# Attention and two MLP layers on one core: one column of the MLP moved out of the attention phase for the first two blocks, and another order of the loads

## The chip, the core and the metric

The kernel runs on one core of one Trainium2 chip. The metric is the time of one execution in microseconds (us) on the device, as the median of several runs. One further execution is taken with the hardware profiler; all durations below come from it.

The engines are TensorE (PE: matrix products; PEld is its loading of weights), VectorE (DVE), ScalarE (ACT), GpSimd (POOL) and SyncE (SP). SP computes nothing here: it issues every transfer between HBM and the core's memory, one after another in its queue.

## What is computed

An attention over a window of 16 positions plus 24 block summaries, then two MLP layers, all in float32:

```
q, k, v: (2, 8, 768, 64)                      # sequences, heads, positions, head size
k_sum = k.reshape(B, H, 24, 32, D).max(3);  v_sum = v.reshape(B, H, 24, 32, D).mean(3)
local   = scale * q @ k.T, masked to |i - j| < 16
summary = scale * q @ k_sum.T + log(32)
a = softmax(concat(local, summary));  x = a @ concat(v, v_sum)     # -> 1536 tokens x 512
h = x @ w_in;   x = softplus(h) @ w_out           # layer 1, 512 -> 2048 -> 512
h = x @ w2_in;  out = relu(h)**2 @ w2_out         # layer 2, the same sizes
```

## The kernel before, in words

**Tiles and blocks.** The 1536 tokens are 12 tiles of 128; tiles 0 to 5 belong to the first sequence, 6 to 11 to the second. Two tiles make a block of 256 tokens. The hidden size of a layer is cut into 16 columns of 128.

**An MLP step** takes one column for one group of tokens. In `mlp_in` (line 664 is its matmul) 12 matmuls write the hidden values h; ACT and DVE apply the nonlinearity and split the result into a rounded part and a rest (g...h and g...l); in `mlp_out` (line 701) 12 matmuls add the column's share to the accumulators accp and acc. Each float32 product is made of three products of rounded numbers, hence tiles such as wih and wil, xh and xl.

**Phases.** `PH` cuts the 16 columns of a layer into three phases: columns 0 to 3, 4 to 9, 10 to 15. The first phase of layer 1, called phase A here, runs in blocks of 256 tokens while attention still runs: after each two tiles of attention the four columns of that block are queued. The text calls one column of one block an A-step. All later phases run in groups of 512 tokens (a B-step is one column of 512 tokens), and they can begin only when the whole attention is done, since their weights and accumulators lie where attention had its tiles ("late places").

**Attention of a tile t** (`tile_sc`, `tile_px`): scores on PE (line 491, into the tile sc), mask and maximum on DVE (499, 530), subtraction on POOL (532), exponential on ACT (534), sum on DVE (516 to 518), scaling on POOL (536), transposition on PE (547), product with the values in vwin on PE (561), and the splitting into xh and xl (306, 571). sc exists once, s and vwin twice (even and odd tiles).

**What attention needs per sequence.** Queries and keys are loaded in pieces of 256 KB (lines 350 and 382) and transposed on PE (361 and 397). The summaries of the keys (ks, and kaug from it) need all six pieces of the sequence's keys before the first scores of that sequence. The summaries of the values need one load of 1.5 MB into late (line 430), and 24 products on PE (line 439, `vsum_mm`). For each tile two windows of the values are loaded into vwin (line 425). In this layout a row of a query, key or window load is 256 bytes.

**Weights.** For each column two loads of 512 KB go into one of four buffers raw (lines 599 and 602). Then each is converted by four to six instructions on ACT, DVE and POOL (609, 611, 614, 306, 308, 623), which also free the buffer.

**What sets the order.** `Plan` records all operations with a due time, an estimated duration and what they need, and lays them out on the engines by a greedy list schedule before anything runs; the order on each engine is then fixed, and each engine works off its queue in order. Where the plan expects PE to be idle for long it puts matmuls without use into PE's queue (line 857); they run whether PE turns out to be idle or not. In the plan a transfer is one queue with a rate (`kb / 245.0`) and a latency.

## Time and profile before

| | us |
|---|---|
| median of 3 runs | 619.96 (619.87 to 622.35) |
| profiled execution, its own time | 620.8 |
| its span | 619.0 |
| PE busy | 602.5 (97%) |
| DVE busy | 312.1 (50%) |
| ACT busy | 288.2 (47%) |
| POOL busy | 202.0 (33%) |

The span reads in three parts. Up to about 60 us the transfers are busy all the time. From about 56 to 120 us PE and DVE are both nearly full. After that PE works without a gap to the end, apart from the last stores. Attention ends at about 132 us, phase A at about 150 us.

### The profile page before, as it was taken

Reading aid. Unit: us, or ns where it says so; the run is one execution under the profiler, and the core shown is the slowest. Engines: PE = TensorE matmul, PEld = TensorE weight load, DVE = VectorE, ACT = ScalarE, POOL = GpSimd, SP = SyncE. Lnnn points to the kernel's source line nnn. Section 1 sums busy time; section 2 is a strip of 40 time slices with the busy share of each in tenths; the row PEclk is TensorE's granted clock in tenths of the full one; section 3 lists DMA queues with packets and bytes.
Section 4 is the critical chain, followed back from the end, with each engine's and each line's share of the span. In section 5 each row is a group of like instructions: output and inputs, shape, how many; then the busy total and the mean of one; then the engine's idle time right before and its main releaser. Section 6 shows DMA issues by size and latency. Waiting matters only on the chain.

```text
span 619.0 us, 9449 instructions
## 1 busy us (share of the span) xinstructions
PE 602.5 (97%) x3809; PEld 507.5 (82%) x3809; DVE 312.1 (50%) x449; ACT 288.2 (47%) x501; POOL 202.0 (33%) x197
## 2 busy tenths in 40 slices
PE   9798999999999999999999999999999999999996
PEld 7687988999788888888888888888888888888885
DVE  5788999726664133542146652247542533232332
ACT  4686888856653124542247643346412432221220
POOL 5877696535550042331138440116000410000000
PEclk9798999999999999999999999999999999999999
DMA  9999632423541014340024330114100100010011
GB/s 283 243 281 217 162 74 55 116 69 116 166 128 35 0 35 136 103 136 1 0 64 122 120 103 0 35 61 131 47 1 0 69 0 2 0 58 11 20 50 68
DMA packets 64524, 51.34 MB, mean 83 GB/s; under 512 B 36320, under 2 KB 58848, under 8 KB 64480
## 3 DMA queue, kind: packets, MB, share of 16 engines
q1 hardware_dynamic: 64480, 50.73, 28.6%
q8 instruction: 30, 0.49, 0.3%
q14 instruction: 14, 0.11, 0.1%
HBM read 47.58 MB, written 3.15 MB: 82 GB/s over the span
## 4 chain that ended last, share of the span: by engine, by line
PE 84%; DVE 8%; DMA 4%; ACT 2%; SPq 1%; issue 1%; POOL 0%; DVEq 0%; POOLq 0%
PE h L664 40%; PE accp L701 21%; PE acc L701 18%; DMA late<-in_v_dram 2%; DMA vwin<-in_v_dram 2%; DVE raw L614 2%; DVE mx L530 1%; DVE s L499 1%; PE ab L439 1%; PE ab L561 1%; DVE sm L516 1%; SPq L382 1%; PE ab L547 1%; DVE xl L571 0%; DVE sm L517 0%
## 5 line engine op out<-in xcount | busy, mean ns | idle before, releaser
L664 PE MATMUL h<-xh,wih 128*128 128x512 f32 (+1 forms) x432 | 159.9, 370 | 0.0
L664 PE MATMUL h<-xh,wil 128*128 128x512 f32 (+1 forms) x432 | 158.7, 367 | 0.0
L664 PE MATMUL h<-xl,wih 128*128 128x512 f32 (+1 forms) x432 | 158.7, 367 | 0.0
L614 DVE SCALAR_TENSOR_TENSOR raw<-raw 128x512 uint32<-128x512 uint32 x128 | 113.3, 902 | 52.8 <-ACT raw L609 39.8
L664 PEld LDWEIGHTS h<-xh,wih 128*128 128x128 f32 x432 | 81.5, 189 | 14.6 <-issue 0.6
L664 PEld LDWEIGHTS h<-xh,wil 128*128 128x128 f32 x432 | 81.3, 188 | 13.9
L664 PEld LDWEIGHTS h<-xl,wih 128*128 128x128 f32 x432 | 81.4, 188 | 13.7
L673 ACT ACTIVATE e<-h 128x512 f32<-128x512 f32 x48 | 28.8, 599 | 125.4 <-PE h L664 125.4
L675 DVE SCALAR_TENSOR_TENSOR h<-h,e 128x512 f32<-128x512 f32 x48 | 33.5, 698 | 103.2 <-ACT e L673 103.1
L671 ACT ACTIVATE h<-h 128x512 f32<-128x512 f32 (+1 forms) x60 | 29.8, 499 | 83.2 <-PE h L664 83.1
L308 POOL TENSOR_SCALAR wih<-raw 128x512 fp32r<-128x512 f32 x18 | 12.6, 703 | 150.5 <-PE h L664 142.1
L623 POOL TENSOR_TENSOR wol<-raw,woh 128x512 fp32r<-128x512 f32 x30 | 42.6, 1421 | 48.9 <-ACT woh L306 48.3
L623 POOL TENSOR_TENSOR wil<-raw,wih 128x512 fp32r<-128x512 f32 x31 | 42.6, 1374 | 28.9 <-ACT wih L306 27.4
L609 ACT ACTIVATE raw<-raw 128x512 uint32<-128x512 uint16 x59 | 39.3, 670 | 13.2 <-DMA raw<-in_moe_w_out_dram 7.5
L680 DVE TENSOR_TENSOR g1l<-h,g1h 128x512 fp32r<-128x512 f32 (+1 forms) x40 | 24.2, 606 | 31.9 <-ACT g1h L678 31.8
L723 DVE TENSOR_TENSOR part<-accp,part 128x512 f32<-128x512 f32 x24 | 16.0, 686 | 43.5 <-PE accp L701 43.5
L680 DVE TENSOR_TENSOR g2l<-h,g2h 128x512 fp32r<-128x512 f32 x28 | 19.3, 690 | 33.7 <-ACT g2h L678 33.5
L306 ACT ACTIVATE raw<-raw 128x512 f32<-128x512 f32 x41 | 27.5, 673 | 18.7 <-DVE raw L614 18.7
L680 DVE TENSOR_TENSOR g0l<-h,g0h 128x512 fp32r<-128x512 f32 (+1 forms) x40 | 24.1, 605 | 21.1 <-ACT g0h L678 20.9
L678 ACT ACTIVATE g0h<-h 128x512 fp32r<-128x512 f32 (+1 forms) x40 | 21.2, 534 | 16.4 <-DVE h L675 16.0
L536 POOL TENSOR_TENSOR s<-s,sm 128x960 f32<-128x960 f32 (+1 forms) x14 | 22.1, 1580 | 13.9 <-DVE sm L518 13.0
L678 ACT ACTIVATE g1h<-h 128x512 fp32r<-128x512 f32 (+1 forms) x40 | 21.4, 534 | 9.2 <-DVE h L675 8.9
(172 smaller groups left out, 1175.4 us busy)
## 6 DMA issues: line engine op xcount, KB each, us to landing
raw<-in_moe_w_in_dram SPq DMA_DIRECT2D x32, 512.0 KB, 4.2
raw<-in_moe_w_out_dram SPq DMA_DIRECT2D x32, 512.0 KB, 3.4
vwin<-in_v_dram SPq DMA_DIRECT2D x20, 192.0 KB, 5.7
part<-in_k_dram SPq DMA_DIRECT2D x12, 256.0 KB, 4.9
late<-in_v_dram SPq DMA_DIRECT2D x2, 1536.0 KB, 11.3
out_dram<-part SPq DMA_DIRECT2D x12, 256.0 KB, 2.1
part<-in_q_dram SPq DMA_DIRECT2D x10, 256.0 KB, 5.1
vwin<-in_v_dram SPq DMA_DIRECT2D x4, 160.0 KB, 5.2
```

What stands on the lines that cost most here:

```text
L306: nc.scalar.activation(out=out_, in_=in_, func=AF.Copy, **({} if mul is None else {"scale": mul}))
L536: op(("POOL", "DVE"), (1.8 * n + 0.1, 1.75 * n), due, lambda e, sv=sv, rv=rv, spread=spread: tt(e).tensor_tensor(out=sv, in0=sv, in1=sprea ...
L609: nc.scalar.activation(out=lo, in_=q4[:, :, 1], func=AF.Copy, scale=2.0 ** -13, bias=-4095.5 / 8192.0)
L614: nc.vector.scalar_tensor_tensor(out=lo, in0=hi, scalar=n, in1=lo, op0=how, op1=ALU.bitwise_or)
L623: op(("POOL", "DVE"), (1.4, 1.0), dv, lambda e: tt(e).tensor_tensor(out=ws[s][kl], in0=lo.bitcast(F32), in1=ws[s][kh].bitcast(F32), op=ALU ...
L664: nc.tensor.matmul(out=hview(st), lhsT=ws[s][wn][:, w_], rhs=xx[bl][:, kk, o:o + n], start=(kk == 0 and xx is xh and wn == "ih"), stop=(kk ...
L671: op("ACT", ta, due, lambda: nc.scalar.activation(out=hview(st), in_=hview(st), func=AF.Softplus), w=[H_], tab="sp")
L673: op("ACT", ta, due, lambda: nc.scalar.activation(out=e_t[st["g"] % 2], in_=hview(st), func=AF.Relu), r=[H_], w=[("e", st["g"] % 2)])
L675: op("DVE", tv, due, lambda: nc.vector.scalar_tensor_tensor(out=hview(st), in0=hview(st), scalar=0.0, in1=e_t[st["g"] % 2], op0=ALU.max, o ...
L678: op("ACT", ta, due, lambda: nc.scalar.activation(out=gview(st)[0], in_=hview(st), func=AF.Copy), r=[H_] + need, w=gk[0])
L680: op("DVE", tv, due, lambda: nc.vector.tensor_tensor(out=gview(st)[1], in0=hview(st), in1=gview(st)[0].bitcast(F32), op=ALU.subtract), r=[ ...
L701: nc.tensor.matmul(out=o, lhsT=a[:, sl], rhs=b, start=(st["first"] and c == 0 and not (A and m % 2)), stop=(st["last"] and c == 2 and not ...
```

## The change

- `FA = (3, 3, 4, 4, 4, 4)`: in phase A blocks 0 and 1 do columns 0, 1 and 2 only. Column 3 of these 512 tokens becomes the first step of the second phase of layer 1.
- `EARLY` goes from 2 to 1: only the loads of column 0's weights get the early due time.
- `REL_K`, `REL_D`: in the plan the keys of the second sequence may not be issued before 24, 28 and 32 (the plan's own time), per pair of pieces.
- The plan's estimates of transfers change (latency, and the sizes that stand for pieces with short rows), and two copies (`vsum_put`, `mk_kaug`) go through the common helper; the copy of the value summaries may now also be put on ACT. With these the whole list schedule comes out in another order, the number of matmuls without use too.

The core of the diff (a new style "d" of the softmax in `tile_sc` and a list `KAUG_E` with POOL alone are left out: no tile uses the one, and the other is what stood there):

```diff
 PH = ((0, 4), (4, 10), (10, 16))
+FA = (3, 3, 4, 4, 4, 4)
...
-EARLY = 2
+EARLY = 1
...
+REL_K = 24.0
+REL_D = 4.0
+REL_V = 0.0
...
             if kb:
-                dma = max(dma, end + 1.6) + kb / 245.0
-                end = dma + 0.3
+                dma = max(dma, end + 1.2) + kb / 245.0
+                end = dma + 1.5
...
             for t0 in range(0, NT, n):
+
+                if L == 1 and ph < 2:
+                    f0, f1 = (0, FA[t0 // 256]) if A else (FA[t0 // 256], PH[1][1])
                 for f in range(f0, f1):
...
-        T += 24 * 0.2267 * st["n"] / 512 + (13.0 / PH[0][1] if st["A"] and st["t0"] < 1024 else 0.0)
+        T += 24 * 0.2267 * st["n"] / 512 + (13.0 / FA[st["t0"] // 256] if st["A"] and st["t0"] < 1024 else 0.0)
...
-    def ld_qk(src, u, place, due):
+    def ld_qk(src, u, place, due, rel=0.0):
...
-                w=[(place, r)], kb=285)
+                w=[(place, r)], kb=285, rel=rel)
...
-                w=[(place, z)], kb=180)
+                w=[(place, z)], kb=206)
...
-            out=PL["V"], in_=v[b].rearrange("h (p r) d -> p h r d", r=VR)), w=["V"], kb=1017)
+            out=PL["V"], in_=v[b].rearrange("h (p r) d -> p h r d", r=VR)), w=["V"], kb=1090, rel=b * REL_V)
...
-        op("POOL", 1.3, due, lambda: nc.gpsimd.tensor_scalar(
...
+        op(("POOL", "ACT"), (1.15, 1.0), due, lambda e: copy(
...
-            (ld_qk if b else ld_pair)(k, u, K_AT[u], dk - LD_K[b])
+            if b:
+                ld_qk(k, u, K_AT[u], dk - LD_K[b], REL_K + REL_D * (u - NU))
+            else:
+                ld_pair(k, u, K_AT[u], dk - LD_K[b])
...
-            run_steps(stA[nA * blocks:nA * blocks + nA], LAG_A)
+            run_steps([st for st in stA if st["t0"] == 256 * blocks], LAG_A)
```

What this does to the queues, at three places. Line numbers in rows of the changed kernel are its own: 358, 433, 438, 611 and 614 there are 350, 425, 430, 599 and 602 here on SP; 369, 447, 497 and 676 there are 361, 439, 491 and 664 here on PE. raw are weights, late is the value load for the summaries, vwin the windows of the values, part the place of queries and keys.

First, the loads of SP behind the first keys and queries. Before:

```order
L599 DMA raw_75<-in_moe_w_in_dram 128x4x256
L602 DMA raw_76<-in_moe_w_out_dram 128x1024
L599 DMA raw_77<-in_moe_w_in_dram 128x4x256
L602 DMA raw_78<-in_moe_w_out_dram 128x1024
L430 DMA late<-in_v_dram 128x8x384
```

Now:

```order
L611 DMA raw_75<-in_moe_w_in_dram 128x4x256
L614 DMA raw_76<-in_moe_w_out_dram 128x1024
L438 DMA late<-in_v_dram 128x8x384
L433 DMA vwin_130<-in_v_dram 80x8x64
L433 DMA vwin_130<-in_v_dram 96x8x64
L611 DMA raw_77<-in_moe_w_in_dram 128x4x256
```

The first value load stands behind two weight loads instead of four.

Second, further down SP's queue, up to the last key piece of the second sequence. Before (the late load here is the second sequence's):

```order
L350 DMA part_69<-in_q_dram 128x8x64 x2
L350 DMA part_70<-in_k_dram 128x8x64 x2
L350 DMA part_69<-in_q_dram 128x8x64 x2
L599 DMA raw_75<-in_moe_w_in_dram 128x4x256
L430 DMA late<-in_v_dram 128x8x384
L602 DMA raw_76<-in_moe_w_out_dram 128x1024
L599 DMA raw_77<-in_moe_w_in_dram 128x4x256
L425 DMA vwin_130<-in_v_dram 96x8x64 x2
L602 DMA raw_78<-in_moe_w_out_dram 128x1024
L350 DMA part_70<-in_k_dram 128x8x64
L425 DMA vwin_131<-in_v_dram 96x8x64 x2
L350 DMA part_70<-in_k_dram 128x8x64
```

Now:

```order
L438 DMA late<-in_v_dram 128x8x384
L358 DMA part_70<-in_k_dram 128x8x64 x2
L614 DMA raw_76<-in_moe_w_out_dram 128x1024
L433 DMA vwin_130<-in_v_dram 96x8x64 x2
L358 DMA part_70<-in_k_dram 128x8x64 x2
L611 DMA raw_77<-in_moe_w_in_dram 128x4x256
L433 DMA vwin_131<-in_v_dram 96x8x64 x2
L614 DMA raw_78<-in_moe_w_out_dram 128x1024
L358 DMA part_70<-in_k_dram 128x8x64
L611 DMA raw_75<-in_moe_w_in_dram 128x4x256
L433 DMA vwin_130<-in_v_dram 96x8x64 x2
L358 DMA part_70<-in_k_dram 128x8x64
```

All six key pieces now stand behind the value load, among the windows of tiles 2, 3 and 4, and five weight loads stand ahead of the last piece where it was four.

Third, on PE, the products for the second sequence's value summaries (ab from late and sel). Before, they stood behind the products of tile 2 with its values (ab from at and vwin):

```order
L361 MATMUL ab_141<-ident,part_69 128x128 x4
L561 MATMUL ab_142<-at_134,vwin_130 64x64 x16
L439 MATMUL ab_141<-late,sel 24x128 x24
L664 MATMUL h_108<-xh_71,wih_91 128x256
```

Now they stand before column 1 of block 0 (h_109 from wih_87), right behind column 0 and the scores of tile 4:

```order
L676 MATMUL h_108<-xh_71,wil_84 128x256
L497 MATMUL sc<-kaug_128,qT_126 64x120 x16
L369 MATMUL ab_142<-ident,part_69 128x128 x4
L447 MATMUL ab_141<-late,sel 24x128 x24
L369 MATMUL ab_142<-ident,part_70 128x128 x4
L676 MATMUL h_109<-xh_71,wih_87 128x256
```

They moved ahead of three quarters of block 0's work and of the values of tile 2.

## Rows read from the trace of the kernel before

**Rows 1.** The page's 40 slices of the span: busy tenths of the transfers.

```profile
DMA  9999632423541014340024330114100100010011
```

**Rows 2.** Stretches: length; PE, PEld, DVE, ACT, POOL busy; PE clock, DMA share, GB/s.

```profile
36.27:59.92 23.65, 20.09 (x256) 17.40 (x253) 19.27 (x30) 17.45 (x31) 17.47 (x17) 0.93 1.03 263
52.00:54.00 2.00, 2.00 (x44) 1.68 (x44) 2.00 (x2) 1.55 (x3) 1.36 (x2) 0.50 0.86 144
54.00:56.00 2.00, 2.00 (x25) 1.57 (x18) 2.00 (x4) 1.29 (x5) 1.44 (x2) 0.73 0.83 177
56.00:104.00 48.00, 45.44 (x624) 41.67 (x623) 47.30 (x66) 40.39 (x67) 38.00 (x33) 1.00 0.53 123
59.92:69.69 9.77, 9.75 (x109) 9.38 (x107) 9.70 (x15) 7.95 (x14) 6.39 (x7) 1.00 1.09 235
69.69:132.40 62.71, 59.81 (x809) 55.87 (x810) 53.25 (x78) 51.53 (x84) 42.16 (x33) 1.00 0.29 71
149.70:613.00 463.30, 462.73 (x2048) 380.79 (x2047) 194.31 (x271) 179.92 (x307) 105.57 (x90) 1.00 0.17 56
```

**Rows 3.** The chain that ended last: start us, us, what.

```profile
28.65 0.44 PE ab L361 x4
...
31.20 0.44 PE h L547 x4
...
36.51 1.44 PE h L664 x12
...
38.31 12.58 DMA vwin<-in_v_dram
...
107.54 0.98 PE sc L491 x32
...
111.59 1.44 PE accp L701 x12
...
191.68 2.72 PE h L664 x12
194.40 1.36 PE accp L701 x6
```

**Rows 4.** Timeline of PE: start us, us, operation [idle before <-releaser].

```profile
22.00 2.78 PE L439 MATMUL ab<-late,sel 128*24 128x128 f32 x48 [3.33 <-DMA late<-in_v_dram]
...
36.27 0.36 PE L664 MATMUL h<-xh,wih 128*128 128x256 f32 x1
...
57.30 0.93 PE L857 MATMUL h<-ident 128*128 128x256 bf16 x7
...
58.83 1.15 PE L561 MATMUL ab<-at,vwin 120*64 120x64 f32 x32
```

**Rows 5.** Timeline of SP's queue: start us, us, line and load issued.

```profile
35.24 0.46 SPq L430 DMA_DIRECT2D late<-in_v_dram  x1
```

**Rows 6.** Transfers from 20 to 60: GB/s in 40 slices; issues, KB, landing us.

```profile
GB/s 179 167 200 109 228 197 209 242 212 240 225 221 232 220 131 225 156 335 247 322 388 380 344 387 373 291 204 166 268 269 254 206 152 135 164 189 203 212 345 274
...
late<-in_v_dram SPq DMA_DIRECT2D x1, 1536.0 KB, 9.9
```

**Rows 7.** DVE from 69.69 to 132.40, by line: count, busy us, mean ns, idle.

```profile
L614 DVE SCALAR_TENSOR_TENSOR raw<-raw 128x512 uint32<-128x512 uint32 x11 | 11.5, 1048 | 0.0
...
L611 DVE TENSOR_SCALAR raw<-raw 128x512 uint32<-128x512 uint32 x3 | 3.5, 1174 | 0.0
...
L623 DVE TENSOR_TENSOR wol<-raw,woh 128x512 fp32r<-128x512 f32 x1 | 2.3, 2266 | 0.0
```

**Rows 8.** Who PE waited for from 69.69 to 132.40: us, times, longest.

```profile
PE sc L491 <- DVE s L499: 1.1, 2, 0.6
...
PE accp L701 <- DVE g1l L680: 0.5, 1, 0.5
```

**Rows 9.** The page's groups over the span: count, busy us, mean ns, idle before, releaser.

```profile
L614 DVE SCALAR_TENSOR_TENSOR raw<-raw 128x512 uint32<-128x512 uint32 x128 | 113.3, 902 | 52.8 <-ACT raw L609 39.8
...
L623 POOL TENSOR_TENSOR wil<-raw,wih 128x512 fp32r<-128x512 f32 x31 | 42.6, 1374 | 28.9 <-ACT wih L306 27.4
```

More of the change, by code (lines that the diff above doesn't have):

```diff
@@ L40 @@
 PEB = 40.0
+REL_K = 24.0
+REL_D = 4.0
+REL_V = 0.0
+KAUG_E = ("POOL",)
 NS_T = 2
@@ L448, in vsum_put @@
     def vsum_put(x, due):
-        op("POOL", 1.3, due, lambda: nc.gpsimd.tensor_scalar(
-            out=vwin[x][0:NS].rearrange("p j h d -> p j (h d)"),
-            in0=vsum.rearrange("p (o x) -> p o x", o=1).to_broadcast([NS, 2, H * D]),
-            scalar1=1.0, scalar2=1.0, op0=ALU.mult, op1=ALU.mult), r=["vsum", "z"], w=[("vsw", x)])
+        op(("POOL", "ACT"), (1.15, 1.0), due, lambda e: copy(
+            e, vwin[x][0:NS].rearrange("p j h d -> p j (h d)"),
+            vsum.rearrange("p (o x) -> p o x", o=1).to_broadcast([NS, 2, H * D])), r=["vsum", "z"], w=[("vsw", x)])
     def mk_kaug(t, due):
@@ L458, in mk_kaug @@
             us = sorted({min(max((c0 + d - 16) // 128, 0), NTB - 1) for d in (0, 95)})
-            op("POOL", 0.55, due, lambda j=j, c0=c0: nc.gpsimd.tensor_scalar(
-                out=kaug[t % 2][:, :, j, NS:], in0=kT[:, :, c0:c0 + WIN],
-                scalar1=1.0, scalar2=1.0, op0=ALU.mult, op1=ALU.mult),
+            op(KAUG_E, (0.55, 0.45)[:len(KAUG_E)], due, lambda e="POOL", j=j, c0=c0: copy(
+                e, kaug[t % 2][:, :, j, NS:], kT[:, :, c0:c0 + WIN]),
                 r=["z"] + [("kT", u, z) for u in us for z in range(2)], w=[("kw", t % 2, j)])
@@ L469, in tile_sc @@
         style = STYLE[t]
-        pe_mask = style in "mn"
+        pe_mask = style in "mnd"
         scb, sck = (acc_pair, "acc") if t == 1 else (sc, "sc")
@@ L526, in exps @@
                                              **({"accum_out": rv[:, p:p + 1]} if style == "n" else {}))
-                op("ACT", NP * (0.55 if style == "n" else 0.37), due, exps, r=[(sck, hh), *mk],
-                   w=sk + (rk if style == "n" else []), tab="exp")
+                if style == "d":
+                    op("DVE", 1.3 * n, due, lambda hh=hh, sv=sv, mv=mv, spread=spread: nc.vector.tensor_tensor(
+                        out=sv, in0=scv(hh), in1=spread(mv), op=ALU.add),
+                        r=[(sck, hh), *mk], w=sk)
+                    op("ACT", 0.2 + 0.8 * n, due, lambda sv=sv: nc.scalar.activation(out=sv, in_=sv, func=AF.Exp), w=sk, tab="exp")
+                else:
+                    op("ACT", NP * (0.55 if style == "n" else 0.37), due, exps, r=[(sck, hh), *mk],
+                       w=sk + (rk if style == "n" else []), tab="exp")
             else:
@@ L764, in attention @@
             dk = d0 - 8.0 + 0.1 * u if b == 0 else due_t(2 * (u - NU) + 2) + KLAG
-            (ld_qk if b else ld_pair)(k, u, K_AT[u], dk - LD_K[b])
+            if b:
+                ld_qk(k, u, K_AT[u], dk - LD_K[b], REL_K + REL_D * (u - NU))
+            else:
+                ld_pair(k, u, K_AT[u], dk - LD_K[b])
             (tr if b else tr_pair)(k, u, K_AT[u], dk)
@@ L824 @@
     stB = [st for st in steps if not st["A"]]
-    nA = PH[0][1]
     blocks = 0
```

## The prediction

> **What bounds the kernel now.** I read the stretches first. From 149.7 us to the last result PE is busy 462.73 of 463.30 us at full clock [rows 2]: there time is added or taken away only by giving PE more or less work. What another order can win lies ahead of that. The slices of the transfers show 9 in the first four of 40 (some 60 us) and fall after that [rows 1]. In that time PE stands still twice for loads: 3.33 us for the first value load, up to 22.00 [rows 4], and up to 50.9 for the windows of tile 2, on the chain as a transfer of 12.58 us from 38.31 [rows 3]. After the second stop the granted clock is 0.50 from 52 to 54 and 0.73 to 56 [rows 2]: PE spends time at the lower of its two levels (1.2 GHz, not 2.4). From 56 to 104 DVE is busy 47.30 of 48 us and PE 45.44 [rows 2]: both are full. From tile 6's scores at 69.69 to the end of tile 11's values at 132.40, PE is idle 62.71 - 59.81 = 2.9 us [rows 2]. So the order of loads counts up to some 60 us, and after that PE's work, with DVE close behind.
>
> **What is added at the end.** Column 3 of the first 512 tokens becomes one B-step: 2.72 for h and twice 1.36 for the products behind it = 5.44 us [rows 3], on PE, in a stretch without gaps: **+5.44**. In exchange two A-steps go, each 12 matmuls in 1.44 and 12 more in 1.44 us [rows 3], 5.76 together. By work alone the change is worth 0.3 us. The rest hangs on whether phase A ends more than 5.44 us earlier. Behind tile 11's values both orders have the same 14 groups of 12 matmuls of phase A, so what counts is when these values are done, 132.40 before. I follow PE to there in four legs.
>
> **Leg 1, to the first MLP matmul, 36.27 before [rows 4].** The first value load has two weight loads of 512 KB less ahead of it. At about 375 GB/s, as from 40 to 44 us [rows 6], 1.05 MB take 2.8 us, so it lands at about 19.2, not 22.0. But ACT now copies the value summaries ahead of the exponentials of tile 1, so softmax takes part of that back. Bounds: 0 and 2.8 us. I take **-1.1**, nearer the lower end, because the softmax of tiles 0 and 1 did not wait for that load before.
>
> **Leg 2, to the end of tile 3's values, 59.92 before.** The stretch lasts 23.65 us. In it PE is idle 3.56 [rows 2], spends 0.93 on seven matmuls without use [rows 4] and loses 2 x 0.50 + 2 x 0.27 = 1.54 us to the clock [rows 2]. Work at full clock: 17.6 us. The new order has tile 5's scores (0.98) and the second product of column 2 (1.44) in it too, and two transpositions of 0.44 less [rows 3]: 19.1 us. In the way stands the second value load, since its products now come right behind column 0 and tile 4's scores. PE gets there at 35.2 + 1.44 + 0.98 + 0.44 = 38.1. Before, the load was issued at 35.24 and took 9.9 us [rows 5, 6]: it landed at 45.1, 23.1 us behind the first. Between the two there are the same 5.5 MB now, but four pieces with rows of 256 bytes are replaced by two weight loads. The former go at 206 GB/s on average from 20 to 34 us, the latter at 375 [rows 6]; for 1.05 MB that makes 2.3 us less: 19.2 + 20.8 = 40.0. Bounds: 38.8 if the rate of weights holds more widely, and 42.4 if nothing is gained by the mix. Wait 1.9 us, and 0.7 for some time at the lower clock behind it (between 0 and 1.5). The windows of tile 2 come 1.4 MB later, at about 46, and PE asks for them at about 50: that wait goes. Leg: 19.1 + 1.9 + 0.7 = 21.7, **-2.0**.
>
> **Leg 3, to tile 6's scores, 9.77 us before [rows 2].** Now there are 21 matmuls without use (seven take 0.93 [rows 4], so 2.8 us), four transpositions of keys and queries and two of tile 4 (6 x 0.44), columns 0 and 1 of block 1 (2 x 1.44), and 0.3 for changes between them: 8.6 us, **-1.2**. These scores need the last key piece. Behind the value load it has 2.75 MB of short rows, at 180 to 206 GB/s, and 2.1 MB of weights at 375: it lands at 59 to 61, and PE wants it at about 61.7. That wait is hidden, with little to spare. Tile 6 starts 4.3 us earlier, at 65.4.
>
> **Leg 4, to the end of tile 11's values, 62.71 us before [rows 2].** PE has one A-step (2.88) less, tile 4's two transpositions (0.88) are behind it, one query transposition (0.44) is added: **-3.3**. DVE gets lighter by more: up to its last split in attention it loses two L611 (1.17 each), one L623 (2.27) [rows 7] and tile 5's sum, already done: some 6 us. Of PE's 2.9 idle us at least 1.6 are waits for DVE [rows 8]; I take **-1.5**. Bounds: -2.9, and +2 if the new order waits elsewhere, about what one of the two old load waits cost.
>
> Sum: 5.44 - 1.1 - 2.0 - 1.2 - 3.3 - 1.5 = **-3.7 us**. It is made in the profiled execution (620.8 in all, span 619.0) and carried over to the median of 619.96: 616.3.
>
> **At nothing** I cost the conversion of weights (column 3's are now first used by block 2; the others stand as far ahead of their use as before, since phase A moves as a whole), the issue of the moved loads on SP, and the last stores. If the weights of columns 6 to 9 lost that cover, the first B-steps would wait; the gapless stretch [rows 2] shows that they did not before.
>
> **Rivals.** *The lead is lost on the value load.* PE stands in order behind the second value load, with columns 1 and 2 of block 0 and the transpositions of tiles 2 and 3 behind it. If it lands at 42.4, 2.4 us go: 618.7. For it: 109 to 256 GB/s from 20 to 36 us [rows 6]. Against it: fewer short rows.
>
> *DVE does not get lighter.* L623 and L611 go from DVE to POOL and ACT in phase A, three subtractions and four shifts in all. L614 takes 1048 ns in this stretch [rows 7] and 902 over the whole span [rows 9], one L623 on DVE 2266: DVE is stretched where POOL works beside it. If each of the three moved subtractions on POOL (1374 ns [rows 9]) holds DVE up for its whole length, 4.1 of the 6 us come back and the -1.5 of leg 4 is gone: 617.8. The Trainium skill, page "SBUF — State Buffer", section "Who interferes with whom", says that a VectorE instruction with two SBUF inputs and a GpSimd instruction that reads SBUF lock each other out for a whole instruction; L614 is of that kind. By that rule this rival holds; the trace shows L614 stretched, not by whom.
>
> *The keys come too late: slower.* All key pieces of the second sequence stand behind the second value load now. Behind the last one PE still has 3.2 us to do before tile 6's scores. Legs 1 to 3 (4.3 us) turn a net of +0.6 (5.44 - 3.3 - 1.5) into -3.7; they are used up if the piece lands at 65.9, and the kernel is slower by 0.5% from 69 on. If the 4.85 MB behind the value load go at 144 to 177 GB/s, as from 52 to 56 us [rows 2], it lands at about 70, tile 6 starts at 73.5, and the time is 624. Against it: a good part of these bytes are weights, which went at 375.
>
> *More than that.* No time at the lower clock (0.7), leg 1 whole (1.7) and no idle time in leg 4 (1.4) make it 612.5.
>
> **How the numbers follow.** Forecast, 616.3: 0.42. More than that, 612.5: 0.08. Value load late, 618.7: 0.20. DVE not lighter, 617.8: 0.14. Keys late, 624: 0.16. A measurement of this kernel tells about 0.5% (3.1 us) from no change; the forecast lies just beyond it. So faster 0.50, same 0.34, slower 0.16. The range leaves out the far parts of the two end cases: 612.5 to 622.0.
>
> **What would show it.** Tile 6's scores at about 65 and tile 11's values done at about 123 show legs 1 to 4; phase A then ends at about 141. A wait of PE of 1 to 3 us for the second value load, ahead of column 1, is expected; over 3 us it shows the first rival. L614 at 1.2 us or more and waits of PE for DVE as before show the second, a wait for a key piece ahead of tile 6 the third. The scheme as a whole is wrong if PE has gaps behind 132 us, or if the B-step costs other than 5.44.

## The result, and the profile after

The changed kernel is slower: 625.69 us against 619.88, a ratio of 1.0081 with a 95% interval of 1.0061 to 1.0100. The prediction was 616.3, with a range up to 622.0. One of the six executions of the changed kernel, at 3403 us, and one of the four of its repeat further down, at 1208 us, are left out of every ratio; without them the medians are 625.55 and 624.56. Profiled, it takes 625.55 with a span of 623.8; before it was 620.8 and 619.0.

First the stretches of the changed kernel, cut where the prediction cut its legs: the first MLP matmul (37.62), the end of tile 3's values (59.64), tile 6's scores (72.71), the end of tile 11's values (131.68). Columns: length; PE, PEld, DVE, ACT, POOL busy; PE's clock, DMA share, GB/s. They answer to [rows 2].

```profile
37.62:59.64 22.02, 19.35 (x283) 17.18 (x281) 19.55 (x27) 19.01 (x33) 18.66 (x17) 1.00 1.08 236
59.64:72.71 13.07, 10.16 (x73) 8.91 (x70) 10.14 (x16) 9.36 (x16) 9.21 (x9) 0.87 0.88 215
72.71:131.68 58.97, 55.74 (x781) 52.49 (x781) 48.05 (x71) 46.94 (x78) 41.22 (x33) 1.00 0.29 71
66.00:68.00 2.00, 2.00 (x12) 2.00 (x11) 2.00 (x4) 1.48 (x2) 1.36 (x2) 0.50 1.13 277
```

| leg, us | before | after | change | predicted |
|---|---|---|---|---|
| 1, to the first MLP matmul | 36.27 | 37.62 | +1.35 | -1.1 |
| 2, to the end of tile 3's values | 23.65 | 22.02 | -1.6 | -2.0 |
| 3, to tile 6's scores | 9.77 | 13.07 | +3.3 | -1.2 |
| 4, to the end of tile 11's values | 62.71 | 58.97 | -3.7 | -4.8 |
| behind that | 486.6 | 492.1 | +5.5 | +5.44 |
| sum | 619.0 | 623.8 | +4.8 | -3.7 |

The last leg is right. The front, which was to shrink by 9.1 us, shrank by 0.7. The stop for tile 2's windows is gone (from 36 us on PE waits for no load), and with it the lower clock of [rows 2]: leg 2 runs at 1.00. The two large misses are legs 1 and 3. These are PE's main idle times, in its timeline (start, us, operation [idle before <-releaser]), with the first MLP matmul, where leg 1 ends:

```profile
20.54 2.77 PE L447 MATMUL ab<-late,sel 128*24 128x128 f32 x48 [4.79 <-DMA late<-in_v_dram]
37.62 0.36 PE L676 MATMUL h<-xh,wih 128*128 128x256 f32 x1
...
51.03 0.38 PE L713 MATMUL accp<-g1l,woh 128*128 128x256 f32 x1 [1.55 <-DVE g1l L692]
...
61.72 0.66 PE L369 MATMUL ab<-ident,part 128*128 128x128 f32 x4 [0.70 <-DVE ks L377]
65.53 0.93 PE L369 MATMUL ab<-ident,part 128*128 128x128 f32 x4 [2.07 <-DVE xl L583]
...
82.20 1.05 PE L497 MATMUL sc<-kaug,qT 64*64 64x120 f32 x32 [1.55 <-DVE s L505]
94.97 1.05 PE L497 MATMUL sc<-kaug,qT 64*64 64x120 f32 x32 [1.68 <-DVE s L505]
```

The wait for the first value load [rows 4] is still there, 4.79 us up to 20.54. In place of the wait for tile 2's windows [rows 3] there are waits for DVE: for the split of h (g1l), for a key sum (ks), for the split of tile 3 (xl), for two mask additions (s). Behind the 2.07 us for xl the clock is at its lower level (0.50 from 66 to 68), and block 1's first 12 matmuls take 2.6 us instead of 1.44 [rows 3]. What DVE did ahead of three of these waits (L626 joins two halves of a weight, it is L614 of before; L523 is a small step of the softmax sum):

```profile
47.87 2.20 DVE L626 SCALAR_TENSOR_TENSOR raw<-raw 128x512 uint32<-128x512 uint32 x1 [0.31 <-ACT h L683]
63.81 0.87 DVE L523 TENSOR_SCALAR sm<-sm 128x8 f32<-128x8 f32 x1
77.57 3.03 DVE L626 SCALAR_TENSOR_TENSOR raw<-raw 128x512 uint32<-128x512 uint32 x1
```

And POOL at the same times:

```profile
47.74 1.79 POOL L548 TENSOR_TENSOR s<-s,sm 128x960 f32<-128x960 f32 x1
62.87 1.79 POOL L544 TENSOR_TENSOR s<-s,mx 128x960 f32<-128x960 f32 x1 [1.34 <-DVE mx L542]
77.00 1.29 POOL L635 TENSOR_TENSOR wil<-raw,wih 128x512 fp32r<-128x512 f32 x1
78.26 1.78 POOL L544 TENSOR_TENSOR s<-s,mx 128x960 f32<-128x960 f32 x1
```

An undisturbed join takes 0.68 us. The first of these ends at 50.07, 0.54 behind the end of POOL's product (49.53); the last ends at 80.60, 0.56 behind the second of two POOL instructions (80.04). DVE stood still until POOL was done, and then did its half microsecond. The small L523 ends 0.02 behind POOL.

The B-step, on the chain that ended last, costs what it did in [rows 3]:

```profile
163.80 2.74 PE h L676 x12
166.54 1.36 PE accp L713 x6
167.90 1.36 PE acc L713 x6
```

### The profile page after: what moved, and what is told of

Read it like the earlier page. It is cut to its first block, busy times and chain, and to the rows that moved or that the text cites. A ratio compares the mean times of both kernels' runs of the same rounds, so it can differ in the third digit from the quotient of the medians.

```text
span 623.8 us, 9450 instructions
## 1 busy us (share of the span) xinstructions
PE 602.6 (97%) x3807; PEld 506.6 (81%) x3807; DVE 308.5 (49%) x442; ACT 288.0 (46%) x501; POOL 206.7 (33%) x199
## 4 chain that ended last, share of the span: by engine, by line
PE 86%; DVE 5%; DMA 3%; POOL 2%; ACT 1%; SPq 1%; issue 1%; DVEq 0%; POOLq 0%; ACTq 0%
PE h L676 41%; PE accp L713 22%; PE acc L713 18%; DMA late<-in_v_dram 2%; POOL s L548 1%; DMA raw<-in_moe_w_out_dram 1%; PE ab L573 1%; DVE raw L626 1%; DVE s L505 1%; PE ab L559 1%; PE sc L497 1%; SPq L390 1%; DVE mx L542 1%; POOL wil L635 0%; PE ab L447 0%
## 5 line engine op out<-in xcount | busy, mean ns | idle before, releaser
L626 DVE SCALAR_TENSOR_TENSOR raw<-raw 128x512 uint32<-128x512 uint32 x128 | 118.4, 944 | 38.0 <-ACT raw L621 19.2
L316 POOL TENSOR_SCALAR wih<-raw 128x512 fp32r<-128x512 f32 x20 | 14.8, 741 | 158.6 <-PE h L676 149.7
L635 POOL TENSOR_TENSOR wol<-raw,woh 128x512 fp32r<-128x512 f32 x32 | 44.7, 1399 | 33.4 <-ACT woh L314 32.6
L635 POOL TENSOR_TENSOR wil<-raw,wih 128x512 fp32r<-128x512 f32 x32 | 43.6, 1363 | 18.7 <-ACT wih L314 17.0
L621 ACT ACTIVATE raw<-raw 128x512 uint32<-128x512 uint16 x63 | 42.0, 676 | 6.0 <-DMA raw<-in_moe_w_out_dram 5.3
L314 ACT ACTIVATE raw<-raw 128x512 f32<-128x512 f32 x46 | 30.9, 673 | 26.7 <-DVE raw L626 26.6
L690 ACT ACTIVATE g1h<-h 128x512 fp32r<-128x512 f32 (+1 forms) x40 | 21.3, 533 | 16.2 <-DVE h L687 15.8
L548 POOL TENSOR_TENSOR s<-s,sm 128x960 f32<-128x960 f32 (+1 forms) x14 | 23.4, 1673 | 7.6 <-DVE sm L524 4.5
L690 ACT ACTIVATE g0h<-h 128x512 fp32r<-128x512 f32 (+1 forms) x38 | 20.5, 543 | 10.2 <-DVE h L687 9.9
```

The lines of the kernel that those rows point to most:

```text
L314: nc.scalar.activation(out=out_, in_=in_, func=AF.Copy, **({} if mul is None else {"scale": mul}))
L548: op(("POOL", "DVE"), (1.8 * n + 0.1, 1.75 * n), due, lambda e, sv=sv, rv=rv, spread=spread: tt(e).tensor_tensor(out=sv, in0=sv, in1=sprea ...
L621: nc.scalar.activation(out=lo, in_=q4[:, :, 1], func=AF.Copy, scale=2.0 ** -13, bias=-4095.5 / 8192.0)
L626: nc.vector.scalar_tensor_tensor(out=lo, in0=hi, scalar=n, in1=lo, op0=how, op1=ALU.bitwise_or)
L635: op(("POOL", "DVE"), (1.4, 1.0), dv, lambda e: tt(e).tensor_tensor(out=ws[s][kl], in0=lo.bitcast(F32), in1=ws[s][kh].bitcast(F32), op=ALU ...
L690: op("ACT", ta, due, lambda: nc.scalar.activation(out=gview(st)[0], in_=hview(st), func=AF.Copy), r=[H_] + need, w=gk[0])
```

## The experiments

Three questions: which part of the change loses; whether the new waits of PE are the loss; and what PE's work in the front is worth at all. Each time stands beside runs of the kernel before on the same chip, which took 619.9 to 621.1 us (medians); ratios are to these, and kernels measured on different chips are compared by their ratios (0.1% is 0.6 us). "Theory P" is that loads and waits between engines set the front and PE's work does not.

### The parts of the change

The moved column alone, in the kernel before (`FA` and its three uses, nothing else):

```diff
+FA = (3, 3, 4, 4, 4, 4)
```

> The kernel before with nothing but the moved column (FA 3, 3, 4, 4, 4, 4). The tail behind tile 11's values grows to 492 us under every theory. Theory P: the front does not get shorter by the 5.76 us of the two A-steps; tile 11's values end at 129 to 133 (132.4 before), time 622 to 626. Rival K (the order package spoils a gain that the moved column alone would bring): tile 11's values end at 127 or earlier, time 620 or less.

629.26 us, 1.0133 (1.0111 to 1.0156), slower than either theory allowed. Tile 11's values end at 136.8: 4.4 us later than before, though two A-steps (5.76 us) are gone. The plan did not leave the rest alone: between 36 and 137 us it put in 47 matmuls without use (6.0 us) where there were 7 (0.9), and one more group of 12 stands ahead of tile 11's values, which leaves 13 behind them and a tail of 490.1 instead of the expected 492.

Everything else of the change, without the moved column:

```diff
-FA = (3, 3, 4, 4, 4, 4)
+FA = (4, 4, 4, 4, 4, 4)
```

> The changed kernel with column 3 of the first two blocks back in phase A (FA all 4); the held keys, the single early column, the new load model and the shared copy of the value summaries stay. Theory P (phase A's front is set by loads and by the waits between DVE, ACT and POOL, so that two A-steps fewer on PE win little there, while the B-step's 5.44 us come back whole): behind tile 11's values the tail is 486.6 us again, as before, and tile 11's values end between 131.7 (the A-steps fit into gaps) and 137.4 (5.76 us of matmuls come back in full); time 620 to 626, and nearer 620 if the gaps were free. Rival K (the held keys and the new order of loads are the loss, whatever column 3 does): tile 11's values end behind 136 and the time stays at 624 or more.

627.15 us, 1.0102 (1.0080 to 1.0125); tile 11's values end at 137.5 and the tail is 487.5. Taken alone this is what rival K expected. But the first half alone is slower than both together, and the second is no faster (the intervals overlap), so neither can be called the loss by this. The reason is that both halves enter the plan's due times: in these kernels the order of the queues differs from 50 us on at the latest, and PE's waits with it. Two rows of PE, from the moved column alone and then from the rest alone:

```profile
56.57 0.66 PE L364 MATMUL ab<-ident,part 128*128 128x128 f32 x4 [2.25 <-ACT at L309]
```

```profile
61.41 1.23 PE L871 MATMUL sc<-ident 128*128 128x256 bf16 x5 [2.54 <-DVE s L505]
```

So no term can be read off by undoing a part: a new order of the plan can make the front 4.4 us longer with two A-steps less in it.

The keys not held back:

```diff
-REL_K = 24.0
-REL_D = 4.0
+REL_K = 0.0
+REL_D = 0.0
```

> The changed kernel without the hold on the second sequence's keys (REL_K and REL_D 0). Theory P: the keys are not what PE waits for ahead of tile 6, so freeing them wins nothing; the key pieces come ahead of the second value load and of weights again, PE waits for those instead, and the time is 624 to 630. Rival K (the held keys come too late and cost the 3.3 us of leg 3): tile 6's scores come at about 69 to 70 and the time falls to 621 to 623.

628.17 us, 1.0110 (1.0083 to 1.0136): without the hold it is no faster. But this too is another order, with tile 6's scores at 85.9, so it does not show alone that the hold costs nothing.

One conversion held back in the plan:

```diff
-        op(("ACT", "DVE"), (0.75, 0.85), dv, three, w=[RL], rel=due - HOLD)
+        op(("ACT", "DVE"), (0.75, 0.85), dv, three, w=[RL], rel=58.0 if (c, which) == (3, 1) else due - HOLD)
```

> The changed kernel with one edit: the conversion of column 3's second weight matrix may start only after a planned time of 58, so that it stands on ACT behind the copies and exponentials of tiles 3 and 4 instead of ahead of them. Theory S (a stall in ACT's queue: ACT stands from about 52 to 56 at this conversion, whose load lands at 56, and everything behind it, the exponentials of tile 4, the copies of tile 3, then DVE's split of tile 3, comes some 2 us late, which makes PE wait 2.07 us for that split and then run at the lower clock): PE's wait for tile 3's split goes or falls under 0.7 us, block 1's first matmuls run at full clock, tile 6's scores come at 69 to 71 instead of 72.7, and the time is 1.5 to 3.5 us lower, 622 to 624. Rival (DVE is full there and another wait takes the place of this one): tile 6's scores stay behind 72 and the time within 1 us of 625.

628.39 us, 1.0118 (1.0087 to 1.0149). PE's wait for tile 3's split fell from 2.07 to 1.03, tile 6's scores stayed at 72.7, and a wait of 3.40 us for another split came at 91.8. Theory S in this form fell, or rather could not be tested in this way.

### One exchange at a time, the order held

The next kernels keep the changed kernel's order on every engine, word for word, and move a few instructions by hand. Their line numbers are 9 higher: L635 is the join L626, L506 the scores L497, L433 the copy of the key summaries L424. First, the changed kernel once more beside them, unedited:

> The changed kernel again, with nothing edited, beside the next three on the same chip. It shows how far two executions of one order differ: the first value load landed between 19.4 and 20.7 us in four kernels whose order is the same up to there, so the first MLP matmul should come between 35.9 and 37.6, and the time at 624 to 627.

624.56 us, 1.0064 (1.0042 to 1.0086), span 622.4. The first MLP matmul comes at 36.68, tile 3's values end at 58.3, tile 6's scores begin at 71.3, tile 11's values end at 130.3. So 1.4 us of the front are chance, two thirds of it in leg 1: the first value load landed at 19.7 here and at 20.5 above. Legs 3 and 4 are the same in both (13.0 and 59.0).

The split of tile 3 ahead of tile 4's sum, on DVE:

```diff
 TENSOR_REDUCE mx<-s 128x8
+TENSOR_TENSOR xl<-ab,xh 128x4x128
 TENSOR_REDUCE sm<-s 128x8
 TENSOR_SCALAR sm<-sm 128x8
 RECIPROCAL sm<-sm 128x8
-TENSOR_TENSOR xl<-ab,xh 128x4x128
```

> The changed kernel with every engine's order kept but for one exchange on DVE: the split of tile 3 (xl) goes ahead of the sum of tile 4's exponentials (sm) instead of behind it. Nothing else moves. Theory S (leg 3 was lost because this split stood in DVE's queue behind work that was not urgent): PE's wait of 2.07 us for it at 65.5 goes, and with it the stretch at half clock behind it; tile 6's scores come at 69.5 to 71 instead of 72.7, and the time falls by 1.5 to 3.5 us against the control. Rival F (the front is full on all engines, so a wait that is taken away comes back at the next step): the wait goes, tile 11's values still end behind 131 and the time stays within 1 us of the control.

625.21 us, 1.0075 (1.0053 to 1.0097). The wait of 2.07 us is gone, block 1's first 12 matmuls take 1.5 us instead of 2.6, and tile 6's scores begin at 72.6 all the same. PE now waits in two later places:

```profile
68.21 0.62 PE L568 MATMUL ab<-ident,s 128*120 128x128 f32 x4 [1.90 <-POOL woh L325]
72.56 1.05 PE L506 MATMUL sc<-kaug,qT 64*64 64x120 f32 x32 [1.17 <-DVE kaug L433]
```

The reason is that on DVE two joins of weights not needed soon now meet POOL: the first right ahead of a key sum and of the POOL conversion (woh) that the first wait is put down to, the second right ahead of the copy of the key summaries that tile 6 needs:

```profile
65.52 1.95 DVE L635 SCALAR_TENSOR_TENSOR raw<-raw 128x512 uint32<-128x512 uint32 x1
70.60 1.74 DVE L635 SCALAR_TENSOR_TENSOR raw<-raw 128x512 uint32<-128x512 uint32 x1
72.26 0.42 DVE L433 COPY kaug<-ks 128x192 f32<-128x192 f32 x2
```

Then these two joins behind the key sums as well (and on POOL their conversion behind tile 5's product):

```diff
 TENSOR_REDUCE ks<-ab 128x4x4
-SCALAR_TENSOR_TENSOR raw<-raw 128x512
 ...
-SCALAR_TENSOR_TENSOR raw<-raw 128x512
 COPY kaug<-ks 128x192 x2
+SCALAR_TENSOR_TENSOR raw<-raw 128x512
+SCALAR_TENSOR_TENSOR raw<-raw 128x512
```

> The changed kernel with the split of tile 3 ahead of tile 4's sum, as before, and now also two joins of weights that are needed only after 100 us (column 3's second matrix, column 4's first) behind the key sums and the copies of the key summaries on DVE; on POOL the conversion that hangs on them goes behind tile 5's product. Theory S2 (with the split exchanged, these two joins, which stood still behind POOL for 1.95 and 1.74 us, held the key summaries that tile 6 needs): tile 6's scores come 1.5 to 3 us earlier than with the split alone, at about 70, and the time falls to 621.5 to 623.5. Rival F (yet another wait stands behind them): tile 6's scores at 72 and the time at 624.5 to 625.5.

625.14 us, 1.0068 (1.0045 to 1.0091). The first half of theory S2 held: tile 6's scores begin at 68.6, earlier than in the kernel before. The second half did not: the time is that of the control. The gain lasts for one tile, tile 7's scores come at 76.1 (75.8 in the control):

```profile
68.60 1.05 PE L506 MATMUL sc<-kaug,qT 64*64 64x120 f32 x32 [0.22 <-DVE kaug L433]
...
75.53 0.65 PE L568 MATMUL ab<-ident,s 128*120 128x128 f32 x4 [2.78 <-ACT at L323]
```

Three joins that stood still behind POOL moved behind what PE waits for, on DVE at 48, 78 and 88 us:

```diff
-SCALAR_TENSOR_TENSOR raw<-raw 128x512
 TENSOR_TENSOR s<-sc,mask 128x480
 TENSOR_TENSOR g1l<-h,g1h 128x256
+SCALAR_TENSOR_TENSOR raw<-raw 128x512
```

> The changed kernel with every engine's order kept but for three exchanges on DVE: joins of weight halves (raw from raw and raw), which were caught behind a subtraction or product on POOL and lasted 2.20, 3.03 and 1.94 us instead of 0.68, now stand behind the mask additions (s) and the split of h (g1l) that follow them. POOL's work is the same, only what stands behind a blocked join on DVE is now ahead of it. Theory L (DVE's two-input joins stand still until POOL's running instruction is done, and PE waits for what is queued behind them): the PE waits of 1.55 us at 51.0 (g1l), 1.55 at 82.2 and 1.68 at 95.0 (s) go or fall under 0.4 us, and the time falls by 2.5 to 4.8 us against the control. Rival F (DVE is simply full): the waits move to the next step and the time stays within 1 us of the control.

624.12 us, 1.0051 (1.0036 to 1.0066): 0.8 below the control by the ratios, and not clear of noise, since the intervals overlap. That is what rival F expected. (In this kernel and the next, tile 8's mask additions come so early that they overwrite tile 6's probabilities; the amount of work is the same.) PE's waits of 1.54, 1.52 and 1.70 us became 0.74, none and none, with new ones of 0.93, 0.40 and 0.49. Some 4 us of waits were taken away, and 1.8 came back at other places.

> Both edits of the two kernels above together: the split of tile 3 ahead of tile 4's sum, and the three blocked joins behind what PE waits for. Theories S and L together: 4 to 8 us less than the control, 617 to 621, so that the changed kernel is level with the kernel before or faster. If they share one cover (a stall upstream that both hide), less than the sum of the two single gains. Rival F: within 1 us of the control.

624.14 us, 1.0053 (1.0038 to 1.0068): the two edits together are worth what the second is alone.

The joins again, the third by a smaller step, and in leg 1 tile 1's exponentials and sums ahead of the copies of the value summaries:

```diff
 ACTIVATE s<-sc,mx 128x120 x8
-ACTIVATE vsum<-ab 24x128 x4
 ACTIVATE woh<-raw 128x512
 ACTIVATE s<-accp,mx 128x120 x4
-ACTIVATE raw<-raw 128x512
 ACTIVATE s<-accp,mx 128x120 x4
+ACTIVATE vsum<-ab 24x128 x4
+ACTIVATE raw<-raw 128x512
```

> The changed kernel with a few instructions in another place and nothing left out. In leg 1 both halves of tile 1's exponentials on ACT, and its sums on DVE, go ahead of the copies of the value summaries, which wait for the first value load; in legs 2 to 4 three joins on DVE go behind the mask additions and the split of h. Theory: from the landing of the value load to the first MLP matmul it takes 15 to 16 us instead of 16.5 to 17.1, and the waits for g1l and s go as in the kernel with the joins alone; together 1.5 to 3 us less than the control, 622 to 624. Rival F (each of these waits has another one right behind it): within 1.3 us of the control, as with the joins alone.

624.91 us, 1.0075 (1.0060 to 1.0090), no faster than the control. The first MLP matmul comes at 35.3, 15.6 us behind the landing of the load; in the kernels without this edit it is 15.8 to 17.1, so the edit itself is not shown to win. What is shown is what an early start is worth:

```profile
41.95 1.45 PE L456 MATMUL ab<-late,sel 128*24 128x128 f32 x21 [3.27 <-ACT g1h L699]
```

PE is at the second value load's products 1.3 us earlier than in the control, at 38.7, and stands there until 41.95. The profile puts the wait down to ACT, but the load itself, issued at 32.52 and 9.3 us on its way, landed at 41.8. The next kernel, with the last key piece ahead of tile 4's windows on SP, shows the same by chance of an early first load:

```diff
+DMA part<-in_k_dram 128x8x64
 DMA vwin<-in_v_dram 96x8x64 x2
-DMA part<-in_k_dram 128x8x64
```

> The changed kernel with one exchange on SP: the last key piece of the second sequence is issued ahead of the two window pieces of tile 4 instead of behind them, some 2 us earlier. Theory P: the key was not what tile 6 waited for, so its scores and the time stay within 1 us of the control; the windows come 1 us later, which may cost a little. Rival K (the held keys are late): tile 6's scores and the time come about 2 us earlier.

625.17 us, 1.0078 (1.0060 to 1.0096).

```profile
42.12 1.28 PE L456 MATMUL ab<-late,sel 128*24 128x128 f32 x20 [3.53 <-DMA late<-in_v_dram]
...
73.12 1.05 PE L506 MATMUL sc<-kaug,qT 64*64 64x120 f32 x32 [1.18 <-DVE kaug L433]
```

The first MLP matmul was at 35.36, 2.3 us ahead of the profile at the top, and tile 6's scores begin 0.4 us behind it. The exchange moved the issue of the key piece little, since SP had to wait for its place (55.60 instead of 55.94 us), but it landed at 59.3 instead of 61.7, and that won nothing. In the first profile PE takes this piece only at 68.83, 7 us behind its landing: the rival of late keys is out.

All exchanges together, with nothing left out and no buffer written early:

> The changed kernel with all exchanges together, nothing left out: exponentials and sums of tile 1 ahead of the value summaries, split of tile 3 ahead of tile 4's sum, and joins behind mask additions, splits and key sums. Theory S2 and L together: tile 11's values end at 126 to 128.5 and the time is 618.5 to 621, level with the kernel before. Rival F: 623 to 625.

627.93 us, 1.0117 (1.0087 to 1.0148): slower than the control by 3.3 us by the ratios, and than either theory expected. The time comes back as two large waits, one for ACT, one for a split that stood behind the joins:

```profile
78.90 0.47 PE L568 MATMUL ab<-ident,s 128*120 128x128 f32 x1 [2.82 <-ACT at L323]
94.33 0.39 PE L685 MATMUL h<-xh,wih 128*128 128x256 f32 x1 [2.85 <-DVE g0l L701]
```

### What PE's work is worth, in the front and behind it

The same 46 of the 48 matmuls of two A-steps are left out, in the kernel before and in the changed one; the order stays.

```diff
+                    if thin and (kk, wn, xx) != (0, "ih", xh):
+                        continue
 ...
+            if A and st["c"] == 1 and st["t0"] < 512:
+                return
```

> The kernel before, in its own order, with the same 46 matmuls left out as in the changed kernel (23 of 24 of column 1's A-step in blocks 0 and 1; column 1 of the first 512 tokens is missing from the result): 5.5 us less on PE in the front and no B-step in exchange. This is the half of the change that was to win. Theory P (loads and waits between engines set the front, not PE's work): tile 11's values end 0 to 2 us earlier than 132.4 and the time is 618 to 620. Rival W (PE's work sets it in the kernel before, and only the new order lost that): 4 to 5.5 us earlier, 614.5 to 616.

> The changed kernel in its own order, with most of the matmuls of column 1's A-steps in blocks 0 and 1 left out (1 of 12 for h, 0 of 12 behind it in each block), so that column 1 of the first 512 tokens is missing from the result; 46 matmuls of 0.12 us, 5.5 us of PE, are gone, and everything else on every engine stands where it was. It asks what two A-steps less on PE are worth in the front, which is the term that was to pay for the B-step. Theory P (PE's work does not set the front): tile 11's values end less than 2 us earlier than in the control, measured from the first MLP matmul (93.6 us there). Rival W (PE's work does set it, and only some new stalls hid that): they end 4 to 5.5 us earlier and the time falls to 620 to 621.

The kernel before: 621.30 us, 1.0004 (0.9989 to 1.0018). The changed one: 625.83, 1.0085 (1.0070 to 1.0101). Neither is faster. The stretches from the first MLP matmul to the end of tile 11's values, first the kernel before without that work:

```profile
36.93:131.97 95.04, 85.13 (x1121) 77.12 (x1119) 80.84 (x120) 76.88 (x127) 65.69 (x55) 0.98 0.55 135
```

then the changed kernel without it:

```profile
37.67:132.25 94.58, 80.53 (x1087) 72.72 (x1085) 78.91 (x113) 74.99 (x125) 68.21 (x57) 0.98 0.53 129
```

In the kernel before this stretch has 89.7 us of PE work in 96.1 (the three rows of [rows 2] added); without the steps it has 85.1 in 95.0. The changed kernel has 85.3 in 94.1; without the steps, 80.5 in 94.6. From the first of these four to the last PE has nine microseconds less to do, and the stretch is 1.5 us shorter.

The same from one B-step of the changed kernel, 23 of 24 matmuls (5.2 us) behind 132 us:

```diff
+            if st["c"] == 5 and st["t0"] == 0:
+                return
```

> The changed kernel in its own order, with 23 of the 24 matmuls of one B-step left out (column 5 of the first 512 tokens, 1 of 12 for h and 0 of 12 behind it; that column is missing there from the result), 5.2 us of PE's work behind 132 us, about the same as the 5.5 us that were left out of the front in the two kernels with thinned A-steps. Theory P (behind tile 11's values PE's work is the time, in front of them it is not): 4.8 to 5.4 us less than the changed kernel, 620 to 621. Rival (another engine stands close behind PE there too): less than 3 us.

621.53 us, 1.0014 (0.9998 to 1.0029): 3.1 to 4.2 us below the changed kernel's two series by the ratios, between the 4.8 to 5.4 of theory P and its rival's 3. In the profiles the tail behind tile 11's values is 488.3 us instead of 492.1, 3.8 less. PE's busy time behind 131 us, the changed kernel first:

```profile
131.00:640.00 509.00, 487.76 (x2232) 403.55 (x2228) 206.11 (x288) 190.06 (x330) 112.92 (x97) 1.00 0.18 57
```

```profile
131.00:640.00 509.00, 482.49 (x2198) 398.92 (x2193) 206.90 (x288) 189.84 (x329) 112.88 (x97) 1.00 0.18 57
```

5.27 us less work. The second one's waits of PE behind 140 us (us, times, longest; the changed kernel has 0.3) show that part of it came back, 1.1 us at once (L719 is L713 there):

```profile
PE accp L719 <- ACT part L731: 1.4, 2, 1.1
```

Behind 132 us most of PE's work is time, 3.8 of 5.3 us; ahead of it as much work was worth nothing that can be told from noise.

### POOL's part

POOL's subtraction and product of the attention made into fills of the same tiles, in the changed kernel and in the one before (the probabilities are then not computed):

```diff
-tt(e).tensor_tensor(out=sv, in0=sv, in1=spread(mv), op=ALU.subtract)
+nc.gpsimd.memset(sv, 0.0) if e == "POOL" else tt(e).tensor_tensor(out=sv, in0=sv, in1=spread(mv), op=ALU.subtract)
```

> The changed kernel in its own order, with POOL's subtraction of the maximum and product with the reciprocal replaced by a fill of the same tile, which reads nothing (the attention's probabilities are therefore not computed). DVE's instructions are the same. Theory L (a DVE join that reads two tiles from SBUF stands still while POOL reads SBUF): the joins that lasted 1.9 to 3.0 us behind these POOL instructions fall to 0.7 to 1.4, since only copies and weight splits are left to stop them, and PE's waits for s and g1l behind them go. Rival D (the joins are slow for another reason, such as DVE waiting for its operands): they stay long. For the time: if these stops set the front, 2 to 5 us less than the control; if the front is a web of waits, within 2 us.

> The kernel before, in its own order, with POOL's subtraction and product of the attention replaced by fills that read nothing (probabilities are not computed). Theory X (the new order brought DVE's stops behind POOL onto the path, the old one had them where DVE had time): less than 2 us faster than the kernel before, against 4 us in the changed kernel. Rival Y (the stops cost both kernels the same, so they explain nothing of the difference): 3 to 5 us faster, 615 to 617.

The changed kernel: 621.03 us, 1.0015 (1.0005 to 1.0025), by the ratios 3.0 us below the control and 4.1 below the first series. The kernel before: 619.02, 0.9975 (0.9961 to 0.9988), 1.5 us below the runs beside it. The joins from 36 to 132 us (count; min/median/max ns), the changed kernel and then the one with fills:

```profile
L626 DVE SCALAR_TENSOR_TENSOR raw<-raw x20: 642/1033/3027, 38.3 to 108.9; 128x512 uint32<-128x512 uint32 x20
```

```profile
L626 DVE SCALAR_TENSOR_TENSOR raw<-raw x20: 643/683/1799, 37.2 to 104.5; 128x512 uint32<-128x512 uint32 x20
```

In the kernel before the median falls from 879 to 682 as well. And a join takes its 0.68 us right beside fills, here of the changed kernel:

```profile
92.61 0.68 DVE L626 SCALAR_TENSOR_TENSOR raw<-raw 128x512 uint32<-128x512 uint32 x1
```

```profile
92.13 0.90 POOL L548 MEMSET s<- 128x960 f32 x1
92.97 0.91 POOL L544 MEMSET s<- 128x960 f32 x1
```

So it is POOL's reading that stops the joins, not its being busy. PE's waits for s and g1l are gone in the changed kernel. Tile 6's scores begin at 71.8, no earlier than in the control (71.3); the gain lies behind them. The stretch from the first MLP matmul to tile 11's values takes 90.6 us (93.6 in the control):

```profile
36.70:127.30 90.60, 84.73 (x1133) 78.50 (x1131) 71.53 (x113) 74.99 (x125) 48.28 (x57) 0.98 0.60 141
```

All of it is in leg 4, which took 59.0 us in the control and in which PE now has no idle time left:

```profile
71.80:127.30 55.50, 55.47 (x781) 52.47 (x781) 44.03 (x71) 46.81 (x78) 28.92 (x33) 1.00 0.30 76
```

One reservation: a fill takes 0.90 us where the product takes 1.79, so the softmax itself is shorter too. The two effects are not told apart: what the fills win is what POOL's arithmetic costs in all, and the share of the stops alone is not shown. Moving three stopped joins out of PE's way won 0.8 us, within the noise.

## Why the prediction was wrong

**What bounds the kernel.** The end was read rightly: gapless, and the B-step costs what the chain said. The front was not. I read DVE at 47.30 and PE at 45.44 of 48 us [rows 2] as "both full", and then counted every matmul taken from PE as time. The thinned kernel before shows the error in itself: 5.5 us of PE's work, nearly what the change moves, taken out without anything in exchange, are worth nothing there (the interval allows 0.7 us). ACT's and DVE's part of those steps stays in it, so this speaks of PE alone. From 56 to 104 us DVE is still busy 46.6 of 48 us in it, PE 43.6; that DVE and what it waits for were the longer side is my reading, not shown by a run. **So the failed step is the rule behind the sum of legs 3 and 4, PE's work as length, above all in leg 3, where waits for DVE and the lower clock were put at nothing and came to 4.5 us.** A move that takes work from a stretch where it is covered to one where it is not costs the whole work, 5.44 (the tail grew by 5.5); the change had no other gain of that size. Of the 8.5 us between forecast and result 4.5 are leg 3, 2.5 leg 1, 1.1 leg 4 and 0.4 leg 2.

**Leg 1 (-1.1, measured +1.35, +0.4 in the control).** The load landed at 20.5, not 19.2, and between 19.1 and 21.1 in the fifteen kernels whose loads share this order up to there; the term was sized on one execution of another order. The larger error is the other term. I had the load win 2.8 us and the softmax give 1.7 of them back; it won 1.5, and the way behind it lost 2.8, since from the landing to the first MLP matmul it takes 17.1 us (16.9 in the control) where it took 14.3 [rows 4]. The leg decides little: whether the first MLP matmul came at 35.3 or 37.6, PE was held by the second value load until 42 or by DVE behind it, and tile 6 came at 73.

**Leg 2 (-2.0, measured -1.6, -2.0 in the control).** Right in size, partly for other reasons. The second value load was no wait in the first profile and 2.2 to 3.5 us where leg 1 was short; it landed between 40.1 and 42.2 in the twelve kernels of this order (forecast 40.0). The first rival (a late load) held in kind, not in effect; the rates that speak for it [rows 6] go from 109 to 242 GB/s up to 36 us, not to 256.

**Leg 3 (-1.2, measured +3.3).** This is the largest miss, 4.5 us. My 8.6 us were a list of PE's instructions, with waits and the lower clock at nothing. In the profile the 13.07 us are 2.9 of idle time, nearly all of it the waits for ks and xl, and 10.16 of busy time, 1.6 more than the list; the stretch at the lower clock behind the wait for xl accounts for most of that. PE had two banks (ab) for transpositions, which ACT and DVE empty, and DVE had sums, maxima and weight joins in its queue ahead of that. The runs show how stiff this is rather than one cause: from the second value load's products to tile 6's scores it takes 30.2 to 32.3 us in ten kernels of this order, with PE's steps thinned, with the worst wait exchanged away, with POOL's arithmetic gone. Only the exchange of the split and two joins together shortened it, to 27.9 (29.6 where all exchanges were made), and the next tile gave that back.

**Leg 4 (-4.8, measured -3.7).** As a sum the -3.3 was low: PE is busy 55.74 us in it where it was busy 59.81 [rows 2], 4.1 less. Whether the leg shrank because of that is not shown. DVE has 5.2 us less to do in it too [rows 2]; the thinned kernels take only 1.2 to 1.3 us of PE's work out of this leg and leave its length (62.66 and 59.07); with the fills PE is busy 55.47 of its 55.50 us. The -1.5 for fewer waits failed: PE is idle 3.2 us where it was 2.9, all of it waits for mask additions, 1.1 before [rows 8], because joins stand still behind POOL just ahead of them.

**The rivals.** "DVE does not get lighter" named the mechanism and put it at +1.5. DVE did get lighter, but the sign that was given for this rival came: in leg 4 the same eleven joins take 1337 ns each instead of 1048 [rows 7], 3.0 us more, and PE's waits for DVE did not fall.

```profile
L626 DVE SCALAR_TENSOR_TENSOR raw<-raw 128x512 uint32<-128x512 uint32 x11 | 14.5, 1337 | 0.6 <-POOL raw L316 0.6
```

The rival blamed the weight conversions moved to POOL; the joins are stopped by these and by POOL's softmax instructions alike (77.00 and 78.26 above). The fills bound its size, with the reservation above: up to 4.1 us in the changed kernel and 1.5 in the one before. By the Trainium skill, page "SBUF — State Buffer", section "Who interferes with whom", a VectorE instruction with two SBUF inputs and a GpSimd instruction that reads SBUF exclude each other for a whole instruction. The trace agrees (ends 0.54 and 0.56 us behind POOL's end), and the fills, which read nothing, took it away (median 1033 to 683 ns). "The keys come too late" had the right sign and nearly the right time (624), but not the reason: with the last piece landing earlier nothing changed, and in the profile PE waited for no key piece.

**What stays open.** Why this order needs 31 us from the second value load to tile 6 isn't reduced to one resource: no engine is busy all the time there (DVE 19.55 of 22.02 us in leg 2 and 10.14 of 13.07 in leg 3), and nearly every wait that was taken away was replaced. The transfers' share is 1.08 and 0.88 in these legs, and no run took loads away, so what they do to the order is not tested. That the old order suffers less from POOL is measured; that its order was better placed by design isn't shown, since four other orders of the plan came out above both kernels, by 1.3 to 3.2 us against the changed one by the ratios (the smallest is within the noise).

## What to carry to other kernels

An engine that is 95% busy need not be the bound: before moving its work, leave that work out in the unchanged order and see whether the time falls. Moving work from a stretch with covered waits to a gapless one costs its full length, and is repaid only if the first stretch is bound by that same engine. In a program laid out by a list schedule, compare edits with the order held; else each edit draws a new order, and here one such order made the front 4.4 us longer with two A-steps less in it.

## What the hardware showed that was not expected

- A small step with one input on DVE (L523, 128x8) also stood still behind POOL: 0.87 us instead of 0.17, ending 0.02 behind POOL's end. Only the joins had been thought of. Unlike the joins, it stands still behind fills too: in the changed kernel with fills it takes 0.95 us five times, once from 62.87 to 63.82 beside a fill from 62.90 to 63.80.
- The first value load landed anywhere from 19.1 to 21.1 us in kernels whose loads stand in the same order up to there. No trace of that is left at the end of the attention: 131.3 and 132.1 after a first MLP matmul at 35.3 and 35.4, 130.3 after one at 37.9.
